# One SBUF tile for staging and factor buffers (15 to 20), one PSUM tile per unit, whole places for the split halves, in an attention and two-MoE kernel

## The chip, the cores and the metric

The kernel runs on one core of a Trainium2 chip. The metric is the device time of one execution in microseconds (us); before the change it is 1255.41 us, the median of three runs (1255.03 to 1257.26).

## What is computed

Three stages follow each other; the output of each is the input of the next. Everything is float32; products on TensorE run as three passes of a value split into a high part and a rest ("hi" and "lo").

```python
# attention: 8 batches, 8 heads, 576 positions in chunks of 64, head size 64
scores = scale * q_c @ k_c.T;  attn = exp(scores - max) / (sum + 1e-9)
x = (attn @ v_c)                                  # 4608 tokens x 512
# first MoE: d_ff = 1024
h = x @ w_in;  e = exp(h - max);  solu = h * e / (sum(e) + 1e-9)
x = layernorm(solu, eps=1e-6) * g_ln @ w_out      # 4608 x 512
# second MoE: d_ff = 2048
h = x @ w2_in;  out = (h * sigmoid(h)) @ w2_out
```

## The kernel before

**Stage one** (attention and the first MoE) goes over 36 tiles of 128 tokens. For a tile, `attend`, `weigh`, `moe_in`, `norm` and `turn_ln` run in turn; four tiles make a block, and `moe_out` multiplies a block by `w_out` and stores it to DRAM (`y1d`). Beside this, `convert` stages pieces of the weights through tiles `st_w` (2 buffers) and `cv` (4 buffers), `w2_mix` forms the sums of weight blocks that stage two needs, and `w2_store` writes them to DRAM.

**Stage two** does the second MoE with seven products in place of eight for 2 x 2 blocks, in both its matrices. Tokens come in 6 groups of 768. For the first matrix a group has 8 **units** `u` (blocks of 128 rows), taken in pairs, and a unit has seven **products** p1, p6, p2, p7, p5, p4, p3, each of 6 matmuls of 384 columns (line 822). In a pair each product is done for both units before the next one. The products gather in PSUM at four places: X (p1, p2), Y (p6, p7), W (p5, p3) and V (p4). Sums are drawn off into **factor buffers** `tmp`, places of 128 x 384 in SBUF: `c_p1` (ACT, line 830), `c_u2` and `c_u3` (DVE, reading Y, lines 833 and 836), `c22` (DVE, reading W between p5 and p3, line 846), `c21` (line 854), `c12` (DVE, reading W after p3, line 862). SiLU is applied on ACT, then `g_sum` (line 869) takes four differences of the results, and every result is stored to DRAM (`gd`, line 827). A buffer comes free when its store has landed. There are 15 of them, made from tiles that stage one no longer needs: `st_w` and `cv` give two each, `ys` and `junk` one each. While the first group's inputs sit in five of those tiles, fewer are there.

At the turn from one token group to the next, four sums of the new inputs (`raw_t`, POOL) and seven splits (`s_split`: ACT line 786, then DVE or POOL line 790) replace the inputs `y1s` one by one, as the old group's products finish with them. The halves of `y1s` lie in groups of ten, so that the third split falls into two tiles and takes two instructions on each engine.

The second matrix follows in the same way (`out_product`, line 910: 6 groups, 7 products, 4 pieces of 12 matmuls), fed by `g_load` from DRAM and `g_split` (ACT line 894, DVE line 896); its weights `w2o` are loaded (line 745) while the last token group's products run.

**What sets the order.** A planner (`Steps`) goes through all steps with given lengths, due times, needs and counts of places, and gives every step a time; the program is written out in the order of those times, engine by engine. Due times come from `NOMINAL`, `START` and others at the end of the file; the strings `Y_ON`, `T_ON`, `UNIT_ON`, `LOW_ON` say on which engine a split or a difference runs. On the chip each engine takes its instructions in that order, and waits that are needed for the data are set by the tile framework: by region for SBUF, and for PSUM by whole tile. Y of both units of a pair is one PSUM tile of two banks (`hy`), and W of both another (`hw`).

Of the kernel before, what the change touches and what calls it, by code (L numbers as in the profile page):

```python
# [136 lines left out]
def stage_one(T, way_out, w2_from, tiles=36, per=4, ahead=2):  # L137
# [45 lines left out]
    for t in range(tiles):  # L183
        b, tt = divmod(t, per)
        x = T[t]
        op("moe_in", (t,), ("PE", 2.73, dict(need=wi[0] + [("xs", t)], take=["h"], due=x + 2.73)),
           ("PE", 2.73, dict(need=wi[1], free=["xs"], give=[("h", t)], due=x + 5.5)))
        held = HELD[t] == "H"
        if held:
            op("hold", (t,), ("ACT", 1.12, dict(need=[("h", t)], take=["hs"], free=["h"], due=x + gap - 0.5, give=[("hs", t)])))  # L190
        op("norm", (t,), ("DVE", 1.23, dict(need=[("hs" if held else "h", t)])), ("ACT", 1.3, dict(take=["u"])),
           ("DVE", 1.51, dict(free=["hs"], port=True, give=[("free", t)]) if held else dict(free=["h"], due=x + gap - 0.5)), ("ACT", 1.34, {}), ("DVE", 0.15, {}),
           ("POOL", 0.85, {}), ("ACT", 1.12, dict(give=[("u", t)])))
# [22 lines left out]
def stage_two(step, start, groups=6, NF=8, tiles=36):  # L216
# [28 lines left out]
    mixed = [("mixed", j, right, k) for j in range(NF) for right in (0, 1) for k in range(4)]  # L245
    all_raw = {"st_w": ([("sp", 0, 3)], [("sp", 0, 4), ("rt", 0, 1)]), "cv": (mixed, [("sp", 0, 5)], [("sp", 0, 6), ("rt", 0, 1)], [("sp", 0, 1), ("rt", 0, 2), ("rt", 0, 3)]), "ys": 2 * ([("stored", end_b, 3)],), "junk": ([("turned", tiles - 1, 1)],)}
    for tag, needs in all_raw.items():
        for n, need in enumerate(needs):
            plan("spare", (tag, n), need, ["tmp"] * (1 if tag in ("ys", "junk") else 2))
    plan("raw_places", (0,), mixed)  # L250
# [6 lines left out]
    for p in range(groups):  # L257
# [83 lines left out]
def chunk_attention_moe_moe(ctx: ExitStack, tc: tile.TileContext, qk, v, w_in, w_out, g_ln, w2_in, w2_out, out):  # L341
# [53 lines left out]
    for kind, src in ((0, lambda f: w2_in[f]), (1, lambda f: w2_out[128 * f:128 * f + 128, :])):  # L395
        for j in range(K2 // 2):
            for f in (j, j + K2 // 2):
                pieces.append(("w2", f, kind, src(f)))
    conv, whole = {}, {}

    early = {}

    def conv_load(i):
# [6 lines left out]
        else:  # L410
            st = sb.tile([128, 2 * CW], I32 if wide else F32, tag="st_w", name="st_w", bufs=2)
        if len(src.shape) > 2:
# [4 lines left out]
    def conv_a(i, apart=False):  # L417

        st = conv[i][0]
        if st.dtype == F32:  # L420
            if pieces[i][0] == "w2":
                conv[i][1] = sb.tile([128, 2, CW], I32, tag="cv", name="cv", bufs=4)
            return
# [5 lines left out]
        else:  # L429
            cv = sb.tile([128, 2, CW], I32, tag="cv", name="cv", bufs=4)  # L430
        conv[i][1] = cv
# [39 lines left out]
    def conv_c(i):  # L471
# [50 lines left out]
    def w2_mix(j, right):  # L522
        top, low = whole.pop(j), whole.pop(j + K2 // 2)
        a, b = (top[:, 1, 256 * i:256 * i + 256].bitcast(F32) for i in (0, 1))
# [114 lines left out]
    def norm(t):  # L639
# [15 lines left out]
        yield  # L655
        junk = sb.tile([128, 2, 512], BF16, tag="junk", name="junk")
        nc.scalar.activation(out=junk, in_=u, func=AF.Square, bias=nmu, scale=1.0, accum_out=ss)
# [19 lines left out]
    def moe_out(b, m):  # L677
# [96 lines left out]
    def s_places(n):  # L774
        t = sb.tile([128, 4096], F32R, tag="ln", name="y1s", bufs=4)[:, 0:3840].rearrange("p (i a f) -> p i a f", i=5, a=2)
        for i in range(5):
            o, kk = divmod(5 * n + i, 2)
            if o < 7:
                sy[o, kk] = (t, i)

    def s_split(p, o):
        src = raw(p, FROM[SEVEN[o]])
        (t0, i0), (t1, i1) = sy[o, 0], sy[o, 1]
        runs = [(t0, i0, 0, 2)] if t0 is t1 else [(t0, i0, 0, 1), (t1, i1, 1, 1)]
        for t, i, k, n in runs:
            nc.scalar.activation(out=t[:, i:i + n, 0, :], in_=src[:, k:k + n], func=AF.Copy)
        yield
        for t, i, k, n in runs:
            hi, lo = (t[:, i:i + n, a, :] for a in (0, 1))
            (nc.vector if Y_ON[o] == "D" else nc.gpsimd).tensor_tensor(out=lo, in0=src[:, k:k + n], in1=hi.bitcast(F32), op=ALU.subtract)  # L790

    def spare(tag, _):
        n, bufs = {"ys": (1, 2), "junk": (1, 1), "st_w": (2, 2), "cv": (2, 4)}[tag]
        t = sb.tile([128, n, HW], F32, tag=tag, name="tmp", bufs=bufs)
        tmp.extend(t[:, i] for i in range(n))

# [170 lines left out]
SUM_ON = 'EDEEEDDEEDDDDDDD'  # L967
# [40 lines left out]
```

## Time and profile before

| | before |
|---|---|
| median of 3 runs | 1255.41 us |
| profiled execution, its own time | 1254.76 us |
| its span, first to last instruction | 1252.8 us |
| TensorE matmul busy | 1221.4 us, 98% of the span |
| TensorE weight load busy | 1115.1 us, 89% |
| VectorE / ScalarE / GpSimd busy | 819.2 (65%) / 637.4 (51%) / 431.4 us (34%) |
| mean granted TensorE clock | 0.998 of full speed |
| DMA queue | 243.33 MB, 60.3% of the 16 engines' time |

Busy time of TensorE is the union of pipelined matmuls, so an engine that is busy may still start matmuls more slowly than it could: the count of matmuls that a stretch holds says more than its busy share. In the views, a bracket behind an instruction is the idle time of its engine before it and what ended that. Stage one fills the span up to about 505 us, the products of stage two run to about 903 us (mixed with stage one up to 533 us and with the second matrix from 891 us), and the second matrix from 891 us to the end.

### The profile page before, as it was taken

Reading aid. Unit: us, or ns where it says so; the run is one execution under the profiler, and the core shown is the slowest. Engines: PE = TensorE matmul, PEld = TensorE weight load, DVE = VectorE, ACT = ScalarE, POOL = GpSimd, SP = SyncE. Lnnn points to the kernel's source line nnn. Section 1 sums busy time; section 2 is a strip of 40 time slices with the busy share of each in tenths; the row PEclk is TensorE's granted clock in tenths of the full one; section 3 lists DMA queues with packets and bytes.
Section 4 is the critical chain, followed back from the end, with each engine's and each line's share of the span. In section 5 each row is a group of like instructions: output and inputs, shape, how many; then the busy total and the mean of one; then the engine's idle time right before and its main releaser. Section 6 shows DMA issues by size and latency. Waiting matters only on the chain. (4 is left out here: it accounts for less than half of the span.)

```text
span 1252.8 us, 22744 instructions
## 1 busy us (share of the span) xinstructions
PE 1221.4 (98%) x8535; PEld 1115.1 (89%) x8535; DVE 819.2 (65%) x1304; ACT 637.4 (51%) x1030; POOL 431.4 (34%) x457
## 2 busy tenths in 40 slices
PE   6999999999999999999999999998999999999998
PEld 3777888888888888899999999998899999999998
DVE  7998877889888544376565656573656555555553
ACT  6776755555555547454343434354555444444441
POOL 1432343343433316556464737366650000000000
PEclk9999999999999999999999999999999999999999
DMA  7343554655654414285656565658898777777772
GB/s 294 127 153 114 170 164 161 218 179 193 202 173 161 139 48 145 83 267 199 232 184 227 193 222 186 233 174 281 272 323 281 213 225 211 220 211 217 223 210 87
DMA packets 137645, 244.77 MB, mean 195 GB/s; under 512 B 15168, under 2 KB 92992, under 8 KB 137536
## 3 DMA queue, kind: packets, MB, share of 16 engines
q1 hardware_dynamic: 137536, 243.33, 60.3%
q8 instruction: 67, 1.10, 0.4%
q14 instruction: 42, 0.34, 0.1%
HBM read 143.66 MB, written 99.61 MB: 194 GB/s over the span
## 5 line engine op out<-in xcount | busy, mean ns | idle before, releaser
L896 DVE TENSOR_TENSOR gs<-gs 128x768 fp32r<-128x768 f32 x168 | 165.8, 988 | 142.3 <-ACT gs L894 142.0
L894 ACT ACTIVATE gs<-gs 128x768 fp32r<-128x768 f32 x168 | 142.2, 847 | 176.9 <-PE h L910 61.0
L627 PE MATMUL h<-wi,xs 128*128 128x512 f32 x864 | 214.6, 397 | 1.7 <-ACT hs L637 1.7
L683 PE MATMUL yp<-lnT,wo 128*128 128x512 f32 x864 | 215.1, 398 | 0.0
L627 PEld LDWEIGHTS h<-wi,xs 128*128 128x128 f32 x864 | 159.3, 188 | 37.7 <-ACT hs L637 3.1
L683 PEld LDWEIGHTS yp<-lnT,wo 128*128 128x128 f32 x864 | 157.6, 188 | 32.2
L822 PE MATMUL h<-y1s,w2t 128*128 128x384 f32 x864 | 163.6, 337 | 0.6 <-DVE y1s L790 0.6
L910 PE MATMUL h<-gs,w2o 128*128 128x384 f32 x864 | 162.4, 337 | 0.6 <-DVE gs L896 0.5
L869 POOL TENSOR_TENSOR tmp<-tmp 128x384 f32<-128x384 f32 x96 | 107.7, 1128 | 135.3 <-DVE tmp L869 96.5
L822 PEld LDWEIGHTS h<-y1s,w2t 128*128 128x128 f32 x864 | 152.6, 189 | 1.2 <-DVE y1s L790 0.9
L910 PEld LDWEIGHTS h<-gs,w2o 128*128 128x128 f32 x864 | 152.1, 188 | 1.2 <-DVE gs L896 0.8
L822 PE MATMUL hw<-y1s,w2t 128*128 128x384 f32 x576 | 111.5, 339 | 8.7 <-DVE tmp L846 8.3
L822 PE MATMUL hy<-y1s,w2t 128*128 128x384 f32 x576 | 109.4, 336 | 2.6 <-DVE tmp L836 2.6
L822 PEld LDWEIGHTS hw<-y1s,w2t 128*128 128x128 f32 x576 | 101.2, 189 | 11.9 <-DVE tmp L846 11.3
L910 PE MATMUL hy<-gs,w2o 128*128 128x384 f32 x576 | 107.3, 335 | 0.3 <-DVE gs L896 0.3
L910 PE MATMUL hw<-gs,w2o 128*128 128x384 f32 x576 | 107.5, 336 | 0.0
L822 PEld LDWEIGHTS hy<-y1s,w2t 128*128 128x128 f32 x576 | 100.9, 188 | 4.1 <-DVE tmp L836 3.9
L910 PEld LDWEIGHTS hy<-gs,w2o 128*128 128x128 f32 x576 | 100.4, 188 | 0.8 <-DVE gs L896 0.8
L910 PEld LDWEIGHTS hw<-gs,w2o 128*128 128x128 f32 x576 | 100.9, 188 | 0.0
L612 ACT ACTIVATE lnT<-tp 128x512 fp32r<-128x512 f32 x72 | 42.7, 598 | 77.6 <-PE tp L672 77.6
L614 DVE TENSOR_TENSOR lnT<-tp,lnT 128x512 fp32r<-128x512 f32 x72 | 49.0, 684 | 38.2 <-ACT lnT L612 37.8
L869 DVE TENSOR_TENSOR tmp<-tmp 128x384 f32<-128x384 f32 x96 | 68.7, 729 | 4.9 <-ACT tmp L864 2.5
(128 smaller groups left out, 1640.7 us busy)
## 6 DMA issues: line engine op xcount, KB each, us to landing
gd<-tmp SPq DMA_DIRECT2D x336, 192.0 KB, 2.1
gs<-gd SPq DMA_DIRECT2D x168, 384.0 KB, 3.7
qk<-in_qk_dram SPq DMA_DIRECT2D x36, 512.0 KB, 4.2
st_w<-in_w_out_dram SPq DMA_DIRECT2D x24, 512.0 KB, 4.1
vt<-in_v_dram SPq DMA_DIRECT2D x36, 256.0 KB, 2.7
y1d<-ys SPq DMA_DIRECT2D x36, 256.0 KB, 2.5
ry<-y1d SPq DMA_DIRECT2D x24, 384.0 KB, 4.1
out_dram<-tmp SPq DMA_DIRECT2D x48, 192.0 KB, 3.8
```

Of the source, the lines that this page charges most:

```text
L612: nc.scalar.activation(out=hi, in_=src, func=AF.Copy)
L614: nc.vector.tensor_tensor(out=lo, in0=src, in1=hi.bitcast(F32), op=ALU.subtract)
L627: nc.tensor.matmul(h_t[t][:, n, :], xs[:, a, kk // 2, 128 * (kk % 2):128 * (kk % 2) + 128], wi[b][kk][:, n * 512:(n + 1) * 512], start=(kk ...
L683: nc.tensor.matmul(yp, wo[a][f // 4][:, f % 4, 128 * m:128 * (m + 1)], lnT[b][c][:, f, :], start=(f == 0 and i == 0), stop=(f == K1 - 1 an ...
L822: nc.tensor.matmul(acc, wt[j, o][:, a, kk, :], t[:, i, c, :], start=start and kk == 0 and n == 0, stop=kk == 1 and n == 2, skip_group_chec ...
L869: (nc.vector if T_ON[n] == "D" else nc.gpsimd).tensor_tensor(out=out, in0=in0, in1=in1, op=ALU.subtract)
L894: nc.scalar.activation(out=dst[:, 0], in_=src, func=AF.Copy)
L896: nc.vector.tensor_tensor(out=dst[:, 1], in0=src, in1=dst[:, 0].bitcast(F32), op=ALU.subtract)
L910: nc.tensor.matmul(acc, w[:, a, 128 * i:128 * i + 128], g[:, c, k, :], start=start and kp == 0 and k == 0 and n == 0, stop=kp == NF // 2 - ...
```

## The change

Staging, conversion, output and junk tiles become one SBUF tile `work` of 7680 columns: six parts of 1024 columns serve stage one's loads (2) and conversions (4) with lists of free parts, two of 512 hold `ys`, one holds `junk`. In stage two the same 7680 columns are 20 factor buffers of 384 columns; the first group's inputs take the first ten until they are split. In PSUM, Y and W of one unit now share a tile of two banks (`hyw`, one for even units, one for odd units), in place of Y of both and W of both. Each half (hi, lo) of a split input is one contiguous place of 768 columns, so that every split is one instruction. The planner is told of the new places, of a need of p5 for `c_u3`, and of the two PSUM tiles' last readers in stage one; its numbers at the end of the file are new, and with them the order on all engines.

```diff
-    all_raw = {"st_w": ([("sp", 0, 3)], [("sp", 0, 4), ("rt", 0, 1)]), "cv": (mixed, [("sp", 0, 5)], ...
+    plan("spare", (10, 6), mixed, ["tmp"] * 6)
+    plan("spare", (16, 4), [("stored", end_b, 3), ("stored", end_b, 2), ("turned", tiles - 1, 1)], ["tmp"] * 4)
+    for n, need in enumerate(([("sp", 0, 3)], [("sp", 0, 4), ("rt", 0, 1)], [("sp", 0, 5)], ...
+        plan("spare", (2 * n, 2), need, ["tmp"] * 2)
...
-               ("POOL", 2.1, dict(give=[("sp", p, o)])) if Y_ON[o] == "P" else ("DVE", 1.25 if o != 2 else 1.7, ...
+               ("POOL", 2.1, dict(give=[("sp", p, o)])) if Y_ON[o] == "P" else ("DVE", 1.1, ...
...
-                need += {"p2": [("c_p1", u)], "p7": [("c_u2", u)], "p3": [("c22", u)]}.get(name, [])
+                need += {"p2": [("c_p1", u)], "p7": [("c_u2", u)], "p5": [("c_u3", u)], "p3": [("c22", u)]}.get(name, [])
+                if p == 0 and o == 1 and u < 2:
+                    need.append(("free" if u == 0 else "xs", tiles - 1))
...
+    work = sb.tile([128, 7680], F32, name="work")
+    cv_free, st_free = [0, 1, 2, 3], [4, 5]
+    def part(n, dtype):
+        w = work[:, 1024 * n:1024 * n + 1024]
+        return w if dtype == F32 else w.bitcast(dtype)
...
-        ys = sb.tile([128, BLK], F32, tag="ys", name="ys", bufs=2)
+        n = 6144 + 512 * (m % 2)
+        ys = work[:, n:n + 512]
...
     def s_split(p, o):
         src = raw(p, FROM[SEVEN[o]])
-        (t0, i0), (t1, i1) = sy[o, 0], sy[o, 1]
-        runs = [(t0, i0, 0, 2)] if t0 is t1 else [(t0, i0, 0, 1), (t1, i1, 1, 1)]
-        for t, i, k, n in runs:
-            nc.scalar.activation(out=t[:, i:i + n, 0, :], in_=src[:, k:k + n], func=AF.Copy)
+        hi, lo = sy[o, 0], sy[o, 1]
+        nc.scalar.activation(out=hi, in_=src, func=AF.Copy)
...
+    def spare(n, count):
+        tmp.extend(work[:, HW * i:HW * i + HW] for i in range(n, n + count))
...
-                if at_ not in bank:
-                    bank[at_] = ps.tile([128, 2, 512], F32, tag={"w": "h", "y": "sx"}[at_], name="h" + at_)
-                bank[u, at_] = bank[at_][:, u % 2, 0:HW]
+                if u % 2 not in bank:
+                    bank[u % 2] = ps.tile([128, 2, 512], F32, tag=("h", "sx")[u % 2], name="hyw")
+                bank[u, at_] = bank[u % 2][:, "yw".index(at_), 0:HW]
...
-FIRST = [-128.33, 3, 21.63, 3.75, 5.92, 13.32, 4.31, 12.18, 4.58, 11.93, 5.72, 6.85, 5.13]
-NOMINAL = [sum(FIRST[:t + 1]) + 13.48 * max(0, t + 1 - len(FIRST)) for t in range(36)]
+FIRST = [-83.81, 3, 24.83, 3, 8.92, 13.48, 4.31, 12.84, 4.51, 11.93, 5.72, 6.44, 5.13]
+NOMINAL = [sum(FIRST[:t + 1]) + 13.52 * max(0, t + 1 - len(FIRST)) for t in range(36)]
-W2_FROM = 14
+W2_FROM = 12
-Y_ON = 'PPDDPDP'
-T_ON = 'DDPP'
-UNIT_ON = 'PPPPPDPPPPPPPPPDPPDPDPDPPPDD'
-START = 543.9
+Y_ON = 'PDDDPDP'
+T_ON = 'PDPP'
+UNIT_ON = 'PPPPDDPDPPDPDPDPPPDDDPDPPPDD'
+START = 575.8
-LOW_ON = 'EEEPDDDPPPEPEPDP'
+LOW_ON = 'EEEPDDDPPPEPPPDE'
```

So `g_sum`'s first difference goes from DVE to POOL (three of four run there now), the second split from POOL to DVE (four of seven are on DVE now), and twelve in place of seven of the first weight splits are on DVE.

**First place: TensorE at the turn between two token groups.** The rows are the end of the new group's first pair and the start of its second; `hw` or `hyw` with a DVE wait is p3, `h2` is p1 of the next pair, `hy` or the later `hyw` is p6. Before:

```order
L822 MATMUL h2_7075<-y1s_5703,w2t_5528 128x384 [waits Activation_49]
L822 MATMUL h2_7075<-y1s_5703,w2t_5528 128x384 x5
L822 MATMUL hw_5926<-y1s_5913,w2t_5457 128x384 [waits DVE_49]
L822 MATMUL hw_5926<-y1s_5913,w2t_5457 128x384 [waits Pool_49]
L822 MATMUL hw_5926<-y1s_5913,w2t_5457 128x384 x4
L822 MATMUL h2_7092<-y1s_5703,w2t_5570 128x384 [waits Activation_49]
L822 MATMUL h2_7092<-y1s_5703,w2t_5570 128x384 x5
L822 MATMUL hy_5809<-y1s_5703,w2t_5528 128x384 x6
L822 MATMUL hy_5809<-y1s_5703,w2t_5580 128x384 [waits DVE_49]
L822 MATMUL hy_5809<-y1s_5703,w2t_5580 128x384 x5
L822 MATMUL hw_5926<-y1s_5913,w2t_5506 128x384 [waits DVE_49]
```

With the change:

```order
L829 MATMUL hyw_5648<-y1s_5747,w2t_5304 128x384 [waits DVE_49]
L829 MATMUL hyw_5648<-y1s_5747,w2t_5304 128x384 [waits Pool_49]
L829 MATMUL hyw_5648<-y1s_5747,w2t_5304 128x384 x4
L829 MATMUL hyw_5674<-y1s_5747,w2t_5353 128x384 [waits DVE_49]
L829 MATMUL hyw_5674<-y1s_5747,w2t_5353 128x384 x5
L829 MATMUL h2_6930<-y1s_5546,w2t_5375 128x384 [waits Activation_49]
L829 MATMUL h2_6930<-y1s_5546,w2t_5375 128x384 x5
L829 MATMUL h2_6941<-y1s_5546,w2t_5416 128x384 [waits Activation_49]
L829 MATMUL h2_6941<-y1s_5546,w2t_5416 128x384 x5
L829 MATMUL hyw_5648<-y1s_5546,w2t_5375 128x384 [waits DVE_49]
L829 MATMUL hyw_5648<-y1s_5546,w2t_5375 128x384 x5
L829 MATMUL hyw_5674<-y1s_5546,w2t_5426 128x384 [waits DVE_49]
```

Before, the products of two pairs are mixed here: p6 of the next pair's even unit comes ahead of a DVE step that reads the same tile `hy`, and p6 of the odd unit waits for that step. Now p3 of both units comes first, and each p6 waits for the last reader of its own unit's tile.

**Second place: TensorE within a token group, from p7 to p3 of a pair.** Before:

```order
L822 MATMUL hy_5809<-y1s_5704,w2t_5638 128x384 [waits DVE_49]
L822 MATMUL hy_5809<-y1s_5704,w2t_5638 128x384 x5
L822 MATMUL hy_5809<-y1s_5704,w2t_5748 128x384 x6
L822 MATMUL hw_5926<-y1s_5704,w2t_5718 128x384 x6
L822 MATMUL hw_5926<-y1s_5704,w2t_5748 128x384 x6
L822 MATMUL h2_7334<-y1s_5913,w2t_5718 128x384 x6
L822 MATMUL h2_7344<-y1s_5913,w2t_5910 128x384 x6
```

With the change:

```order
L829 MATMUL hyw_5648<-y1s_5547,w2t_5382 128x384 [waits DVE_49]
L829 MATMUL hyw_5648<-y1s_5547,w2t_5382 128x384 x5
L829 MATMUL hyw_5674<-y1s_5547,w2t_5448 128x384 [waits DVE_49]
L829 MATMUL hyw_5674<-y1s_5547,w2t_5448 128x384 x5
L829 MATMUL hyw_5648<-y1s_5547,w2t_5409 128x384 [waits DVE_49]
L829 MATMUL hyw_5648<-y1s_5547,w2t_5409 128x384 x5
L829 MATMUL hyw_5674<-y1s_5547,w2t_5448 128x384 [waits DVE_49]
L829 MATMUL hyw_5674<-y1s_5547,w2t_5448 128x384 x5
L829 MATMUL h2_7027<-y1s_5747,w2t_5409 128x384 x6
L829 MATMUL h2_7038<-y1s_5747,w2t_5454 128x384 x6
```

The products stand in the same order, but p5, which waited for nothing, now waits for DVE: its tile is the one that `c_u3` reads. Between p7 of a unit and its p5 stands one product of the other unit.

**Third place: TensorE where the second matrix starts** (`gs` rows), from p5 or p4 of the last pair on. Before:

```order
L822 MATMUL h_9158<-y1s,w2t 128x384 x6
L822 MATMUL h_9170<-y1s,w2t 128x384 x6
L910 MATMUL h_9181<-gs,w2o 128x384 x6
L910 MATMUL h_9182<-gs,w2o 128x384 x6
L910 MATMUL h_9181<-gs,w2o 128x384 x6
L910 MATMUL h_9182<-gs,w2o 128x384 x6
L910 MATMUL h_9181<-gs,w2o 128x384 x6
L910 MATMUL h_9182<-gs,w2o 128x384 x6
L822 MATMUL hw<-y1s,w2t 128x384 x6
L910 MATMUL h_9181<-gs,w2o 128x384 x6
L910 MATMUL h_9182<-gs,w2o 128x384 x6
L822 MATMUL hw<-y1s,w2t 128x384 x6
```

With the change:

```order
L829 MATMUL h_8961<-y1s,w2t 128x384 x6
L829 MATMUL h_8973<-y1s,w2t 128x384 x6
L829 MATMUL hyw<-y1s,w2t 128x384 x18
L917 MATMUL h_9014<-gs,w2o 128x384 x6
L917 MATMUL h_9015<-gs,w2o 128x384 x6
L917 MATMUL h_9014<-gs,w2o 128x384 x6
L917 MATMUL h_9015<-gs,w2o 128x384 x6
L829 MATMUL hyw<-y1s,w2t 128x384 x6
L917 MATMUL h_9014<-gs,w2o 128x384 x6
L917 MATMUL h_9015<-gs,w2o 128x384 x6
```

One p3 has moved ahead of the second matrix; the other stands behind 24 of its matmuls.

## Rows read from the trace of the kernel before

**Rows 1.** The profile page, busy time by engine, TensorE:

```profile
PE 1221.4 (98%) x8535; PEld 1115.1 (89%) x8535; DVE 819.2 (65%) x1304; ACT 637.4 (51%) x1030; POOL 431.4 (34%) x457
```

**Rows 2.** Windows, TensorE: stretch, its length, busy (matmuls), clock, DMA share, GB/s.

```profile
592.00:612.00 20.00, 18.36 (x104) 1.00 0.71 244
657.00:677.00 20.00, 18.86 (x107) 1.00 0.69 244
716.00:736.00 20.00, 18.68 (x106) 1.00 0.66 229
778.00:798.00 20.00, 18.88 (x107) 1.00 0.68 242
853.00:891.00 38.00, 33.56 (x181) 0.96 0.77 257
891.00:941.00 50.00, 47.57 (x266) 1.00 0.93 316
1000.00:1020.00 20.00, 20.00 (x117) 1.00 0.81 230
```

**Rows 3.** Waits of TensorE, 500 to 850, then 850 to 940: total, times, longest.

```profile
PE hw L822 <- DVE tmp L846: 2.6, 4, 1.0
PE hy L822 <- DVE tmp L836: 2.6, 4, 0.7
...
PE hw L822 <- DVE tmp L846: 5.6, 3, 3.7
```

**Rows 4.** Timeline of TensorE, 650 to 680: start, length, line, count.

```profile
657.06 3.31 PE L822 MATMUL h<-y1s,w2t 128*128 128x384 f32 x18
660.86 1.31 PE L822 MATMUL hw<-y1s,w2t 128*128 128x384 f32 x6 [0.49 <-DVE tmp L846]
...
664.92 1.33 PE L822 MATMUL hy<-y1s,w2t 128*128 128x384 f32 x6 [0.65 <-DVE tmp L836]
...
667.14 2.26 PE L822 MATMUL h<-y1s,w2t 128*128 128x384 f32 x12
...
673.40 2.24 PE L822 MATMUL h<-y1s,w2t 128*128 128x384 f32 x12
...
677.56 2.26 PE L822 MATMUL h<-y1s,w2t 128*128 128x384 f32 x12
```

**Rows 5.** Timeline of VectorE, the same stretch.

```profile
660.25 0.56 DVE L846 TENSOR_TENSOR tmp<-hw,tmp 128x384 f32<-128x384 f32 x1 [2.08 <-DMA gd<-tmp]
...
664.31 0.56 DVE L836 TENSOR_TENSOR tmp<-hy,tmp 128x384 f32<-128x384 f32 x1 [1.55 <-PE hy L822]
...
675.68 0.56 DVE L854 TENSOR_TENSOR tmp<-h,tmp 128x384 f32<-128x384 f32 x1 [0.48 <-PE h L822]
```

**Rows 6.** Timeline of TensorE, 838 to 945, the passage to the second matrix.

```profile
858.95 2.17 PE L822 MATMUL hw<-y1s,w2t 128*128 128x384 f32 x6 [3.69 <-DVE tmp L846]
...
891.16 6.43 PE L910 MATMUL h<-gs,w2o 128*128 128x384 f32 x36
898.88 1.31 PE L822 MATMUL hw<-y1s,w2t 128*128 128x384 f32 x6 [1.29 <-DVE tmp L846]
...
937.01 2.19 PE L910 MATMUL h<-gs,w2o 128*128 128x384 f32 x11 [0.55 <-DVE gs L896]
```

**Rows 7.** Timeline of VectorE, the same stretch.

```profile
858.33 0.56 DVE L846 TENSOR_TENSOR tmp<-hw,tmp 128x384 f32<-128x384 f32 x1 [6.71 <-DMA gd<-tmp]
...
898.26 0.56 DVE L846 TENSOR_TENSOR tmp<-hw,tmp 128x384 f32<-128x384 f32 x1 [5.06 <-DMA gd<-tmp]
```

**Rows 8.** Instructions of lines 869 and 790: duration in ns, least, median, most.

```profile
L869 DVE TENSOR_TENSOR tmp<-tmp x96: 543/557/2191, 544.6 to 908.0; 128x384 f32<-128x384 f32 x96
L869 POOL TENSOR_TENSOR tmp<-tmp x96: 994/1021/1737, 547.4 to 925.6; 128x384 f32<-128x384 f32 x96
...
L790 DVE TENSOR_TENSOR y1s<-ry,y1s x24: 871/1716/2332, 507.2 to 833.3; 128x384 fp32r<-128x384 f32 x12, 128x768 fp32r<-128x768 f32 x12
```

**Rows 9.** Groups by line and shape: count, busy us, mean ns, idle before.

```profile
L833 DVE TENSOR_TENSOR tmp<-hy,tmp 128x384 f32<-128x384 f32 x48 | 25.6, 553 | 24.4 <-ACT y1s L786 10.9 <-PE hy L822 10.4 <-issue 2.2
...
L614 DVE TENSOR_TENSOR xs<-sx,xs 128x512 fp32r<-128x512 f32 x36 | 24.6, 684 | 6.8 <-ACT xs L612 6.8
```

More of the change, by code (lines that the diff above doesn't have):

```diff
@@ L191, in stage_one @@
         op("norm", (t,), ("DVE", 1.23, dict(need=[("hs" if held else "h", t)])), ("ACT", 1.3, dict(take=["u"])),
-           ("DVE", 1.51, dict(free=["hs"], port=True, give=[("free", t)]) if held else dict(free=["h"], due=x + gap - 0.5)), ("ACT", 1.34, {}), ("DVE", 0.15, {}),
+           ("DVE", 1.51, dict(free=["hs"], port=True, give=[("free", t)]) if held else dict(free=["h"], due=x + gap - 0.5, give=[("free", t)])), ("ACT", 1.34, {}), ("DVE", 0.15, {}),
            ("POOL", 0.85, {}), ("ACT", 1.12, dict(give=[("u", t)])))
@@ L245, in stage_two @@
     mixed = [("mixed", j, right, k) for j in range(NF) for right in (0, 1) for k in range(4)]
[L246 to L249, printed above, removed]
+    plan("spare", (10, 6), mixed, ["tmp"] * 6)
+    plan("spare", (16, 4), [("stored", end_b, 3), ("stored", end_b, 2), ("turned", tiles - 1, 1)], ["tmp"] * 4)
+    for n, need in enumerate(([("sp", 0, 3)], [("sp", 0, 4), ("rt", 0, 1)], [("sp", 0, 5)], [("sp", 0, 6), ("rt", 0, 1)], [("sp", 0, 1), ("rt", 0, 2), ("rt", 0, 3)])):
+        plan("spare", (2 * n, 2), need, ["tmp"] * 2)
     plan("raw_places", (0,), mixed)
@@ L410, in conv_load @@
         else:
-            st = sb.tile([128, 2 * CW], I32 if wide else F32, tag="st_w", name="st_w", bufs=2)
+            conv["st", i] = st_free.pop(0)
+            st = part(conv["st", i], I32 if wide else F32)
         if len(src.shape) > 2:
@@ L421, in conv_a @@
             if pieces[i][0] == "w2":
-                conv[i][1] = sb.tile([128, 2, CW], I32, tag="cv", name="cv", bufs=4)
+                conv["cv", i] = cv_free.pop(0)
+                conv[i][1] = part(conv["cv", i], I32).rearrange("p (a f) -> p a f", a=2)
             return
@@ L429, in conv_a @@
         else:
-            cv = sb.tile([128, 2, CW], I32, tag="cv", name="cv", bufs=4)
+            conv["cv", i] = cv_free.pop(0)
+            cv = part(conv["cv", i], I32).rearrange("p (a f) -> p a f", a=2)
         conv[i][1] = cv
@@ L655, in norm @@
         yield
-        junk = sb.tile([128, 2, 512], BF16, tag="junk", name="junk")
+        junk = work[:, 7168:7680].bitcast(BF16).rearrange("p (a f) -> p a f", a=2)
         nc.scalar.activation(out=junk, in_=u, func=AF.Square, bias=nmu, scale=1.0, accum_out=ss)
@@ L754, in raw_places @@
         if p == 0:
-            for i, tag in enumerate(("st_w", "st_w", "cv", "cv", "cv")):
-                raw_y[i] = sb.tile([128, 2, HW], F32, tag=tag, name="ry0", bufs=2 if tag == "st_w" else 4)
+            for i in range(5):
+                raw_y[i] = work[:, 768 * i:768 * i + 768].rearrange("p (k f) -> p k f", k=2)
         else:
@@ L774, in s_places @@
     def s_places(n):
-        t = sb.tile([128, 4096], F32R, tag="ln", name="y1s", bufs=4)[:, 0:3840].rearrange("p (i a f) -> p i a f", i=5, a=2)
+        t = sb.tile([128, 4096], F32R, tag="ln", name="y1s", bufs=4)[:, 0:3840].rearrange("p (i k f) -> p i k f", i=5, k=2)
         for i in range(5):
-            o, kk = divmod(5 * n + i, 2)
-            if o < 7:
-                sy[o, kk] = (t, i)
+            sy[divmod(5 * n + i, 2)] = t[:, i]
     def s_split(p, o):
         src = raw(p, FROM[SEVEN[o]])
-        (t0, i0), (t1, i1) = sy[o, 0], sy[o, 1]
-        runs = [(t0, i0, 0, 2)] if t0 is t1 else [(t0, i0, 0, 1), (t1, i1, 1, 1)]
-        for t, i, k, n in runs:
-            nc.scalar.activation(out=t[:, i:i + n, 0, :], in_=src[:, k:k + n], func=AF.Copy)
+        hi, lo = sy[o, 0], sy[o, 1]
+        nc.scalar.activation(out=hi, in_=src, func=AF.Copy)
         yield
[L788 to L795, printed above, removed]
+        (nc.vector if Y_ON[o] == "D" else nc.gpsimd).tensor_tensor(out=lo, in0=src, in1=hi.bitcast(F32), op=ALU.subtract)
+    def spare(n, count):
+        tmp.extend(work[:, HW * i:HW * i + HW] for i in range(n, n + count))
     def take(key):
@@ L819, in product @@
         for kk in range(2):
-            t, i = sy[o, kk]
             for n, (a, c) in enumerate(PASSES):
-                nc.tensor.matmul(acc, wt[j, o][:, a, kk, :], t[:, i, c, :], start=start and kk == 0 and n == 0,
+                nc.tensor.matmul(acc, wt[j, o][:, a, kk, :], sy[o, c][:, kk, :], start=start and kk == 0 and n == 0,
                                  stop=kk == 1 and n == 2, skip_group_check=not start)
```

18 lines of the change are left out of this document (11 added, 7 removed).

## The prediction

> **What bounds the kernel now.** The page comes first: TensorE has matmuls in flight for 98% of the span, every other engine 65% at most [rows 1]. Only time in which TensorE starts matmuls late can be won, so the views to read are those that show missing matmuls. In the second matrix a 20 us window holds 117 [rows 2], and 60 of the first matrix take 667.14 to 677.56, 10.42 us: 0.1737 us each [rows 4]. By that pace the four windows at the turns between token groups, with 104, 107, 106 and 107, lack 13 + 10 + 11 + 10 = 44 matmuls, 7.6 us. The stretch 853 to 891 could hold 220 and holds 181: 39 lack, 6.8 us, and its clock is 0.96. From 891 to 941, 266 stand where 289 fit: 23 lack, 4.0 us [rows 2]. Together 18.4 us: all that a change in the order of waits can win in stage two.
>
> The waits name the causes [rows 3]. From 500 to 850 two kinds last, four times each: p3 for `c22`, 2.6 us in all, and p6 for `c_u3`, 2.6 us. The timelines show one turn. `c22` stands 2.08 us on VectorE until a store (`gd`) has landed and its buffer is free [rows 5]; TensorE has p4 of both units and one product more to do in the meantime and then loses 0.49 us [rows 4]. Then p6 of the odd unit waits 0.65 us for `c_u3` [rows 4, 5], which itself waited 1.55 us for p6 of the *next* pair's even unit, since both units share the tile `hy`: a dependence of the tile, not of the data. At the passage `c22` waits 6.71 us and, last, 5.06 us for landings [rows 7]; TensorE loses 3.69 and 1.29 us [rows 6], 5.6 us with a third [rows 3]. After the longest wait six matmuls take 2.17 us, where six after 0.49 or 1.29 us take 1.31 [rows 4, 6]: the granted clock fell, which is most of what the waits alone don't explain of the 6.8.
>
> **Term 1, the turns: 7.6 us, take -5.6.** The way from product to landed store is read at the turn: p5 of that unit ended 6 matmuls before 657.06, at 656.0; the order puts the latest product of the stored result 12 matmuls earlier, at 653.9; the landing was at 660.2 [rows 5]. That is 6.3 us. In the new order the result whose store frees the buffer stands at least 54 matmuls (9.4 us) ahead, counted at all four turns, so the buffer is free 3 us before it is asked for. The wait for `c_u3` goes too: in the first piece of order p3 of both units comes ahead of the new pair's p6, and no step of DVE needs a product behind the one that waits for it. What comes next: p6 of a new unit now waits for `c12` of the old one, its tile's last reader, and in a turn DVE has four splits instead of three, each from 0.87 to 2.33 us [rows 8]. TensorE has one to two products (1.04 to 2.08 us) of other work before it needs `c12`. If a split lies ahead of it the stall is 0 (a 0.87 us split) to about 1.2 us (2.33); I take 0.5 per turn, since about half the splits are short, 2.0 in all: -5.6, ends -7.6 and -2.8.
>
> On that lengthening: the least and median of those splits, 871 and 1716 ns, and VectorE's differences, 543 to 2191 ns [rows 8], differ with the same form of instruction, while the sums that read PSUM average 553 ns over 48 [rows 9]. The Trainium skill, SBUF — State Buffer, section "Who interferes with whom", has a rule for it: a VectorE instruction with two SBUF inputs and a GpSimd instruction that reads SBUF exclude each other for a whole instruction. The trace agrees; by that rule alone, every split that meets a GpSimd operation would take the long time, the stall would be 1.2 in each turn, and the total 2.8 us higher than mine.
>
> **Term 2, 853 to 891: 6.8 us, take -6.3.** Here stores land later. For the last `c22`, p5 ended 18 matmuls before 891.16, at 888.0, and the landing was at 898.2 [rows 6, 7]: 10.2 us from a result with no matmul between. For the first, the stall began at 858.95 - 3.69 = 855.26, p5 ended 18 matmuls earlier at 852.1, and the stored result stands 24 to 30 matmuls (4.2 to 5.2 us) before that: 10.4 to 11.4 us. The new order puts 60 to 114 matmuls there, 10.4 to 19.8 us, and p4 of the pair still covers 2 us. So the two waits go, and with them the fall of the clock; 0.5 us I leave for one landing that is late. Ends -6.8 and -3 (stores slower by a third: one wait stays).
>
> **Term 3, 891 to 941: 4.0 us, take -1.6 + 1.0.** The last `c22` asks for a result 30 matmuls back, and p3, behind 24 matmuls of the second matrix and a p3, waits for it 30 later: 10.4 us against 10.2 and 0.6 for `c22` and its hand-over. The 1.29 us wait shrinks to some tenths and the restart goes with it: -1.6. But the DMA share here is 0.93 [rows 2] and the second matrix already waits 0.55 us for its inputs [rows 6]: what is won before 891 brings the same bytes (w2o, `gd`, `gs`) closer together. Transfers of the 50 us at 0.93 leave 3.5 us of slack; about 12 us are taken out of the time before. Ends 0 and +8 (rival one); I take +1.0, because only the `gs` loads of the first group lie on the path and the loads of w2o before them now start earlier too.
>
> **Term 4, the new wait of p5: take +0.7.** In the second piece of order p5 waits for `c_u3` of its own unit. From p7's end there is one product of room, 1.04 us. The way takes 0.20 us to VectorE (twelve matmuls from 673.40 end at 675.48, the reader starts at 675.68), 0.56 for the sum [rows 4, 5], 0.05 back (664.31 + 0.56 to 664.92): 0.81. So 0.23 us remain, 24 pairs, two units each. Whatever stands in VectorE's way for over 0.23 us is a stall. VectorE has 48 x 0.557 us of differences less than before, which went to POOL at 1.021 us each [rows 8]; I take 0.03 us per pair. Ends 0 and 24 x 0.8 = 19 (rival two). The Trainium skill, PSUM — Partial Sum Buffer, section "PSUM bank collisions raise a hardware error", asks for a guard by bank; p5's half of the tile is another bank than the one that `c_u3` reads, so by it the 0.7 would fall away. The order shows the wait for the whole tile all the same; no row here shows a guard by bank.
>
> **Term 5, stage one: take +0.8.** The order now has only eight transposes between the last `attend` and `moe_in` of an early tile, where more stood before. ACT and then VectorE split what `moe_in` needs; VectorE's part is 0.684 us [rows 9], ACT's I take as as long, with two hand-overs of 0.2: 1.8 us. No row gives the eight transposes alone; between all of the way hidden (0) and none (1.8) I take 0.8, once; ends 0 and 2.
>
> **At nothing:** staging parts in one tile (the same loads and conversions beside a full TensorE, whose list up to 50 us is unchanged); whole places for halves (one split instruction fewer on ACT and one fewer on VectorE or POOL per turn); the number of matmuls (equal); POOL's 48 x 1.02 us more, at 34% busy [rows 1], as long as the differences stay behind `c12` on the path; the second matrix behind 941, whose waits keep over 3 us of room in the order.
>
> **Sum.** -5.6 - 6.3 - 1.6 + 1.0 + 0.7 + 0.8 = -11.0. The profiled execution took 1254.76 us (span 1252.8), so 1243.8; the median of runs stands 0.65 above it: **1244.4 us**.
>
> **Rivals.**
> *One: the passage is bound by DMA.* At a share of 0.93 [rows 2] the saved 8 us before 891 come back as waits for `gs` and w2o after it; terms 1, 4 and 5 remain: -5.6 + 0.7 + 0.8 = -4.1, about 1251. For it: 316 GB/s against 230 to 257 elsewhere. Against: the share falls to 0.77 just before, and loads can move there. Chance 0.12.
> *Two, slower: `c_u3` late within the groups.* With two units in a tile, each pair exposes two chains of 0.81 us to a VectorE that also runs splits and differences, which POOL stretches to 2.19 us [rows 8], and POOL has 49 us more. If TensorE loses 0.8 us in each of 24 pairs, that is +19 on -11: 1263. It decides when `c_u3` starts over 0.23 us late; the kernel becomes slower when the mean lateness passes 0.23 + 11/24 = 0.69 us. Against: within a group no wait of TensorE lasts now [rows 3], and `c_u3` starts freely. Chance 0.08.
> *Three: the turns stay.* Splits on VectorE hold `c12` by 1.2 us or more and p6 with it; the turns win 1 or 2 us in place of 5.6, 1248 to 1249. For it: four of seven splits there. Chance 0.13.
> *Four: it doesn't do what it says.* If landings, not the count of buffers, set the pace, more buffers only shift the wait: 1255. Against: POOL and VectorE have room [rows 1], stores wait for no buffer. Chance 0.05.
>
> **How the numbers follow.** The forecast has 0.62. Its best case takes term 1 to 3 nearly whole and 4 and 5 at nothing, -16.5: 1238.9, a little lower with the spread of the runs: 1237. Upward the range takes in rivals one and three and stops at 1253, leaving rivals two and four and their neighbours out. A measurement of this kernel can tell some 0.2%, 2.5 us, from no change. Faster by more: forecast, one and three, less their upper ends, 0.85; same 0.08; slower 0.07.
>
> **What would show it.** Right: windows at the turns with 114 matmuls or more, no wait of `c22` for `gd` at turns, clock 1.00 in the passage, p5's waits for `c_u3` below 1 us in all. Wrong: p5 or p6 with waits of half a us in most pairs (two); `gs` and w2o waits of several us after the start of the second matrix (one); p6 waiting for `c12` behind a `y1s` split (three); `c22` still behind `gd` (four).

## The result, and the profile after

The changed kernel takes 1238.23 us (median of 4 runs, 1237.28 to 1239.64), the kernel before in the same series 1256.01 us (4 runs, 1255.03 to 1257.26): a ratio of 0.9859, 95% interval 0.9842 to 0.9876. The forecast was 1244.4 us with a range of 1237 to 1253; the gain is 17 to 18 us where 11 were expected. The profiled execution took 1239.64 us, span 1237.5, which is 15.1 us under the profiled execution before.

The page of the changed kernel, busy time by engine (beside [rows 1]):

```profile
PE 1218.4 (98%) x8535; PEld 1115.8 (90%) x8535; DVE 815.5 (66%) x1262; ACT 638.2 (52%) x1024; POOL 467.8 (38%) x493
```

TensorE's busy time hardly moved, 3 us; the count of matmuls in a stretch shows the gain. Windows of TensorE in the changed kernel, the stretches of [rows 2] and one more:

```profile
592.00:612.00 20.00, 19.99 (x115) 1.00 0.76 268
657.00:677.00 20.00, 20.00 (x116) 1.00 0.63 233
716.00:736.00 20.00, 20.00 (x117) 1.00 0.68 251
778.00:798.00 20.00, 20.00 (x116) 1.00 0.65 240
853.00:891.00 38.00, 36.00 (x198) 0.96 0.88 294
891.00:941.00 50.00, 50.00 (x289) 1.00 0.93 304
520.00:540.00 20.00, 20.00 (x103) 1.00 0.42 128
```

The turns are full (117 is the most). 853 to 891 lacks 22 of 220; 891 to 941 is full, and its DMA share is still 0.93. The last window was not priced: before it reads

```profile
520.00:540.00 20.00, 19.45 (x98) 1.00 0.42 123
```

so 5 matmuls, 0.9 us, were won there: before, the first group's products waited 0.6 us for a split of `y1s`, and now they don't. Waits of TensorE from 500 to 940 in the changed kernel (who waited for whom: total, times, longest), beside [rows 3]; it is the whole list:

```profile
PE hyw L829 <- DVE work L853: 2.0, 1, 2.0
```

No p5 waits for `c_u3`, no p6 for `c12`. VectorE's timeline at the turn that [rows 5] showed before (it now comes some 4 us earlier), start and length in us, with the idle time and its end in the bracket:

```profile
651.27 0.56 DVE L843 TENSOR_TENSOR work<-hyw,work 128x384 f32<-128x384 f32 x1 [2.52 <-PE hyw L829]
...
653.37 0.56 DVE L853 TENSOR_TENSOR work<-hyw,work 128x384 f32<-128x384 f32 x1 [0.50 <-PE hyw L829]
...
655.45 0.56 DVE L853 TENSOR_TENSOR work<-hyw,work 128x384 f32<-128x384 f32 x1 [0.48 <-PE hyw L829]
```

For `c_u3` (L843) and both `c22` (L853) VectorE now stands idle until TensorE's product is done, 2.52, 0.50 and 0.48 us; before, TensorE stood for them. The one wait left is at the passage. TensorE, VectorE, GpSimd and the DMA queue of SyncE there:

```profile
861.41 2.24 PE L829 MATMUL hyw<-y1s,w2t 128*128 128x384 f32 x12
...
873.96 2.27 PE L829 MATMUL hyw<-y1s,w2t 128*128 128x384 f32 x12
878.23 1.31 PE L829 MATMUL hyw<-y1s,w2t 128*128 128x384 f32 x6 [2.00 <-DVE work L853]
879.38 5.90 PE L917 MATMUL h<-gs,w2o 128*128 128x384 f32 x24
```

```profile
862.65 0.56 DVE L869 TENSOR_TENSOR work<-hyw,work 128x384 f32<-128x384 f32 x1 [0.48 <-PE hyw L829]
...
865.24 1.35 DVE L876 TENSOR_TENSOR work<-work 128x384 f32<-128x384 f32 x1 [0.99 <-POOL work L876]
...
877.62 0.56 DVE L853 TENSOR_TENSOR work<-hyw,work 128x384 f32<-128x384 f32 x1 [4.50 <-DMA gd<-work]
```

```profile
863.17 4.44 SPq L761 DMA_DIRECT2D w2o<-w2od  x7
867.70 2.57 SPq L834 DMA_DIRECT2D gd<-work  x4
...
872.15 1.74 SPq L834 DMA_DIRECT2D gd<-work  x3
```

The `c22` of the last pair's even unit waits 4.50 us for a landing. Its buffer holds a second difference (865.24, after GpSimd's first), whose p3 ended six matmuls behind 861.41, at 862.45. Counted in the order, its store is the second of the three issued from 872.15, at 872.87, behind seven loads of `w2o`, four stores and a load of `gs`, and it landed by 877.57: 15.1 us from product to landing, where 10.2 to 11.4 were read before. The difference was done at 866.59, 4.1 us behind the product; 6.3 us passed until the store was issued, and 4.7 until it had landed. What the issue stood for is one of those loads: the one issued at 866.67 landed at 872.80, 0.07 us before the store was issued. SyncE's waits from 867 to 874 say the same (total, times, longest):

```profile
SPq L834 <- DMA w2o<-w2od: 2.0, 4, 1.1
```

TensorE loses 2.0 us, and the 24 matmuls after it take 5.90 us, where 24 from 892.42 on take 4.33. From 880 to 900 the window holds 109 at a granted clock of 0.93, a mean of the clock's two levels (1.2 and 2.4 GHz). Together 22 matmuls, 3.8 us.

### The profile page after: what moved, and what is told of

Its sections match the earlier page's. It is cut to its first block, busy times and chain, and to the rows that moved or that the text cites. A ratio compares the mean times of both kernels' runs of the same rounds, so it can differ in the third digit from the quotient of the medians.

```text
span 1237.5 us, 22712 instructions
## 1 busy us (share of the span) xinstructions
PE 1218.4 (98%) x8535; PEld 1115.8 (90%) x8535; DVE 815.5 (66%) x1262; ACT 638.2 (52%) x1024; POOL 467.8 (38%) x493
## 4 chain that ended last, share of the span: by engine, by line
PE 95%; DVE 3%; DMA 1%; ACT 1%; issue 0%; POOL 0%; SPq 0%; DVEq 0%; ACTq 0%; POOLq 0%
PE hyw L917 16%; PE yp L698 16%; PE h L642 16%; PE hyw L829 16%; PE h L917 12%; PE h L829 12%; PE tp L687 2%; PE sx L588 2%; PE sx L595 1%; PE pp L620 1%; DMA w2o<-w2od 0%; DMA gd<-work 0%; DVE e L607 0%; ACT hs L652 0%; DMA qk<-in_qk_dram 0%; DVE mx L605 0%
## 5 line engine op out<-in xcount | busy, mean ns | idle before, releaser
L829 PE MATMUL hyw<-y1s,w2t 128*128 128x384 f32 x1152 | 215.3, 336 | 2.0 <-DVE work L853 2.0
L917 PE MATMUL hyw<-gs,w2o 128*128 128x384 f32 x1152 | 210.9, 335 | 0.0
L829 PEld LDWEIGHTS hyw<-y1s,w2t 128*128 128x128 f32 x1152 | 201.8, 188 | 3.2 <-DVE work L853 2.3
L917 PEld LDWEIGHTS hyw<-gs,w2o 128*128 128x128 f32 x1152 | 200.9, 188 | 0.2 <-issue 0.2
L876 POOL TENSOR_TENSOR work<-work 128x384 f32<-128x384 f32 x144 | 161.0, 1136 | 77.8 <-ACT work L871 67.9
L616 POOL TENSOR_TENSOR e<-e,sm 128x512 f32<-128x512 f32 x36 | 40.5, 1124 | 76.1 <-DVE sm L614 67.3
L855 ACT ACTIVATE work<-work 128x384 f32<-128x384 f32 x48 | 25.2, 524 | 84.4 <-DVE work L853 84.3
L876 DVE TENSOR_TENSOR work<-work 128x384 f32<-128x384 f32 x48 | 52.0, 1091 | 15.6 <-POOL work L876 15.6
L843 DVE TENSOR_TENSOR work<-hyw,work 128x384 f32<-128x384 f32 x48 | 26.5, 555 | 54.0 <-PE hyw L829 54.0
L549 POOL TENSOR_TENSOR work<-work 128x256 f32<-128x256 f32 x64 | 50.4, 808 | 29.0 <-DVE work L497 27.8
```

The lines of the kernel that those rows point to most:

```text
L549: nc.gpsimd.tensor_tensor(out=out_, in0=in0, in1=in1, op=op)
L616: nc.gpsimd.tensor_tensor(out=e, in0=e, in1=sm.to_broadcast([128, HP, 2, CH]), op=ALU.mult)
L829: nc.tensor.matmul(acc, wt[j, o][:, a, kk, :], sy[o, c][:, kk, :], start=start and kk == 0 and n == 0, stop=kk == 1 and n == 2, skip_group ...
L843: nc.vector.tensor_tensor(out=take((u, "u3")), in0=bank[u, "y"], in1=c_t[u, "u2"], op=ALU.add)
L876: (nc.vector if T_ON[n] == "D" else nc.gpsimd).tensor_tensor(out=out, in0=in0, in1=in1, op=ALU.subtract)
L917: nc.tensor.matmul(acc, w[:, a, 128 * i:128 * i + 128], g[:, c, k, :], start=start and kp == 0 and k == 0 and n == 0, stop=kp == NF // 2 - ...
```

## The experiments

All times stand beside runs of the kernel before on the same chip (its medians there were 1255.45 us for the first four kernels below, 1256.36 for the next three and 1256.72 for the last three).

**The parts one by one, planned with the numbers of before.** Three kernels have the changed code with `START`, `FIRST`, `NOMINAL`, `W2_FROM`, `Y_ON`, `T_ON`, `UNIT_ON` and `LOW_ON` of before. The first is that alone:

```diff
-START = 575.8
+START = 543.9
-T_ON = 'PDPP'
+T_ON = 'DDPP'
...
```

> The changed kernel with the numbers and engine strings of before (START, FIRST, Y_ON, T_ON, UNIT_ON, LOW_ON): 20 buffers and one PSUM tile per unit alone, planned anew. Theory A (the waits for landed stores go because more buffers are there): no buffer is asked for less than 11 us behind the product of its stored result at the turns, and 13 us at the passage; so no wait of c22 for gd, about 1235 to 1239 us, as fast as the change or up to 3 us faster. Theory B (the new numbers are what pays): about 1250. Theory C (both are needed): 1242 to 1246.

Measured: 1236.68 us, ratio 0.9851 (0.9836 to 0.9866). Theory A held: no `c22` makes TensorE wait, and the passage is full.

```profile
853.00:891.00 38.00, 38.00 (x221) 1.00 1.02 351
891.00:941.00 50.00, 49.29 (x279) 1.00 0.90 297
```

The new numbers bring nothing that can be seen; the tiles alone give the whole gain. The second has 15 buffers:

```diff
-    plan("spare", (10, 6), mixed, ["tmp"] * 6)
-    plan("spare", (16, 4), [("stored", end_b, 3), ("stored", end_b, 2), ("turned", tiles - 1, 1)], ["tmp"] * 4)
+    plan("spare", (10, 2), mixed, ["tmp"] * 2)
+    plan("spare", (16, 3), [("stored", end_b, 3), ("stored", end_b, 2), ("turned", tiles - 1, 1)], ["tmp"] * 3)
```

> As the run with 20 buffers and the numbers of before, but with 15 buffers (5 more parts of the tile lie idle): the PSUM tile per unit alone. Theory A: c22 takes buffers 3.1 us behind the product at each turn where a landing takes 6.3, so the waits stay or grow, and p5 and p6 now wait behind c22 too: 1254 to 1266 us. Theory that the tile of PSUM pays (the wait of p6 for c_u3, 0.65 us with its restart at each turn): 1249 to 1252.

Measured: 1249.61 us, 0.9958 (0.9944 to 0.9973). Theory A is wrong in one half here. Windows of this kernel at two turns and at the passage:

```profile
657.00:677.00 20.00, 20.00 (x116) 1.00 0.69 254
716.00:736.00 20.00, 20.00 (x117) 1.00 0.71 262
...
853.00:891.00 38.00, 34.29 (x186) 0.95 0.70 229
891.00:941.00 50.00, 46.50 (x260) 1.00 0.95 320
```

The turns are full with 15 buffers: the PSUM tile per unit is enough for them. Theory A's other half did come: `c22` still waits for a landed store at four turns, 1.1 to 1.5 us, and the order still puts p1 of the next pair ahead of p3. At one turn, VectorE, then TensorE:

```profile
656.25 0.56 DVE L853 TENSOR_TENSOR work<-hyw,work 128x384 f32<-128x384 f32 x1 [1.15 <-DMA gd<-work]
```

```profile
654.89 3.31 PE L829 MATMUL h<-y1s,w2t 128*128 128x384 f32 x18
```

These 18 matmuls (p4 of one unit, p1 of the next two) cover it; p3 of both units comes next, and only then p6, so that no p6 stands for a `c_u3`. The passage is as bad as before. VectorE and TensorE there:

```profile
849.06 0.56 DVE L843 TENSOR_TENSOR work<-hyw,work 128x384 f32<-128x384 f32 x1 [7.38 <-DMA gd<-work]
```

```profile
849.67 4.95 PE L829 MATMUL hyw<-y1s,w2t 128*128 128x384 f32 x18 [2.32 <-DVE work L843]
```

18 matmuls take 4.95 us, where 18 at a turn take 3.31 [rows 4]: the clock again. The third has 20 buffers and the PSUM tiles of before:

```diff
-                if u % 2 not in bank:
-                    bank[u % 2] = ps.tile([128, 2, 512], F32, tag=("h", "sx")[u % 2], name="hyw")
-                bank[u, at_] = bank[u % 2][:, "yw".index(at_), 0:HW]
+                if at_ not in bank:
+                    bank[at_] = ps.tile([128, 2, 512], F32, tag={"w": "h", "y": "sx"}[at_], name="h" + at_)
+                bank[u, at_] = bank[at_][:, u % 2, 0:HW]
...
-                need += {"p2": [("c_p1", u)], "p7": [("c_u2", u)], "p5": [("c_u3", u)], "p3": [("c22", u)]}.get(name, [])
+                need += {"p2": [("c_p1", u)], "p7": [("c_u2", u)], "p3": [("c22", u)]}.get(name, [])
```

> As the run with 20 buffers and the numbers of before, but with the PSUM tiles of before (Y of both units, W of both) and without the planner's need of p5 for c_u3: the buffers alone. Theory A: the order has no p6 behind a c_u3 of the same tile any more, since the pairs need not be mixed when buffers are there: 1235 to 1240 us. Theory that the tile of PSUM is half of it: waits of p6 for c_u3 stay at four turns, 1240 to 1244.

Measured: 1239.63 us, 0.9879 (0.9861 to 0.9897). Its windows:

```profile
657.00:677.00 20.00, 20.00 (x117) 1.00 0.64 238
716.00:736.00 20.00, 20.00 (x117) 1.00 0.66 243
...
853.00:891.00 38.00, 38.00 (x219) 1.00 1.00 336
891.00:941.00 50.00, 48.18 (x273) 1.00 0.90 292
```

The turns are full here too: with buffers at hand the planner no longer mixes two pairs, and no p6 stands behind a `c_u3` of the same tile. One wait of 0.7 us for a `c22` is left, at 555 us, within the first group. With one of 0.6 us for a split of `y1s` and 1.9 us for `gs` (0.4 with the tile per unit), it covers most of the 3.0 us that this kernel lies above the first. So either part alone clears the four turns' windows, and only the buffers clear the passage (the kernel before differs from the other three in its staging tiles and in its third split too):

| with the numbers of before | Y of both, W of both | one tile per unit |
|---|---|---|
| 15 buffers | 1255.45 (before) | 1249.61 |
| 20 buffers | 1239.63 | 1236.68 |

**The wait that is left.** One kernel only puts the first difference back on VectorE:

```diff
-T_ON = 'PDPP'
+T_ON = 'DDPP'
```

> The changed kernel with the first difference of g_sum back on VectorE (DDPP), all else as changed. Theory: the one wait left, 2.0 us of c22 for a store at the passage with the fall of the clock behind it (22 matmuls, 3.8 us), comes from the first difference waiting on GpSimd behind splits of w2o, which holds the second difference and its store; then the passage is full, 1234 to 1236 us. Rival (the transfers at a DMA share of 0.94 hold the store): same wait, within 1 us of the change. Second rival: VectorE's 48 differences more make c12 late at the turns: slower by 1 to 4 us.

Measured: 1236.08 us, 0.9844 (0.9827 to 0.986). The passage is full, but something comes back behind it:

```profile
853.00:891.00 38.00, 38.00 (x220) 1.00 0.99 342
891.00:941.00 50.00, 48.85 (x277) 1.00 0.88 288
```

22 matmuls won, 12 lost, 1.7 us by the pace. Seven `w2o` loads stand in the queue here as well; but the planner, given earlier differences, hands this `c22` another buffer, whose product lies some 40 us back. So it is not shown that GpSimd's difference was late, only that the buffer was. The other way is to move the loads:

```diff
+        if 28 <= pos < 42:
+            need = need + [("t", NF * groups - i, n) for i in (3, 4) for n in range(4)]
```

> The changed kernel with seven loads of w2o (the third batch) planned behind the four differences of the last pair but one, so that its stores go ahead of them on the DMA queue; T_ON stays PDPP. Theory (the last wait of c22 comes from the queue: seven loads of 256 KB stand before the store that frees its buffer): the wait of 2.0 us and the fall of the clock go, 22 matmuls or 3.8 us in the passage; some 1 to 2 us may come back as waits for gs: 1235 to 1237 us against 1238.2. Rival (the first difference on GpSimd is late): the wait stays at 1 to 2 us, 1237 to 1239.

Measured: 1239.99 us, 0.987 (0.9853 to 0.9887), a miss in the total: not faster than the change. But its first half held. Windows:

```profile
853.00:891.00 38.00, 38.00 (x221) 1.00 0.92 309
891.00:941.00 50.00, 46.62 (x256) 0.97 0.90 295
```

Waits of TensorE, 500 to 940:

```profile
PE hyw L919 <- DVE work L944: 2.5, 1, 2.5
PE hyw L919 <- DVE gs L905: 0.9, 2, 0.5
```

With the queue in another order and the first difference still on GpSimd, the stores of the pair before land in time and the passage is full, though the planner now hands this `c22` a buffer asked for only 54 matmuls, 9.4 us, behind its product: the loads ahead of the store were enough to make it late. The price came some 40 us later: the draw-off of the second matrix (`o_sum`, L944) stands on VectorE behind `gs` splits that wait for late loads, TensorE loses 2.5 us, the clock falls, and 33 matmuls are gone.

**What comes back behind the passage.** The kernel with `DDPP`, and the last four `w2o` loads later:

```diff
+        if pos >= 48:
+            need = need + [("od", 0, 1, 3)]
```

> The run with DDPP, and the last four w2o loads (needed some 48 us after the second matrix starts) planned behind its second product. Theory (the 12 matmuls, 2.1 us, that 891 to 941 lacks with DDPP are waits for gs behind w2o on the queue, which is what the saved time gave back): they go in part, 1234 to 1235.5 us against 1236.1. Rival (gs is late because its stores gd land late, not because of w2o): no change, 1235.8 to 1236.5.

Measured: 1235.43 us, 0.9834 (0.9817 to 0.985). The window 891 to 941 holds 281 in place of 277: 0.7 us, and the medians differ by as much. But they come from two chips, and the intervals of the two ratios overlap, so the gain is not clear of noise. Of two waits for `gs`, 0.96 and 0.17 us, one of 1.04 us stays: it is not shown that `w2o` was the longer one's cause.

**Whole places for the halves**, undone:

```diff
-        nc.scalar.activation(out=hi, in_=src, func=AF.Copy)
+        runs = [slice(0, 2)] if o != 2 else [slice(0, 1), slice(1, 2)]
+        for k in runs:
+            nc.scalar.activation(out=hi[:, k], in_=src[:, k], func=AF.Copy)
...
```

> The changed kernel with the third split of y1s in two instructions on each engine as before, in the order as planned. Theory: whole places alone bring nothing, since the turns have room: within 0.7 us of the change (1237.5 to 1239). Rival (the turns are short of VectorE time): c12 late and p6 with it at five turns, 1 to 3 us slower.

Measured: 1236.68 us (1235.99 to 1239.71), 0.9848 (0.983 to 0.9866): no slower, so whole places bring nothing. It came out 0.8 us under the range expected, and why leads to the next point: its profile has the same wait, and the window after it a clock of 1.00:

```profile
PE hyw L832 <- DVE work L856: 1.8, 1, 1.8
```

```profile
880.00:900.00 20.00, 20.00 (x116) 1.00 0.90 297
```

**The change and two faster variants on one chip.**

> The changed kernel itself, beside the two fastest variants on the same chip. Theory: its runs lie on two levels about 2 us apart, 1237.3 and 1239.4, by whether the last wait of c22 (about 2 us) is followed by a fall of the granted clock; the mean against the kernel before is 0.985 to 0.987.

Measured: 1238.58 us, 0.9855 (0.9838 to 0.9872); its four runs are 1237.33, 1237.82, 1239.35 and 1239.44. The profiled one, 1239.35, has the same wait of 1.8 us, and then

```profile
880.00:900.00 20.00, 20.00 (x108) 0.92 0.84 269
```

8 matmuls less than in the kernel above with an equal wait: after it the clock fell in one and not in the other, and 8 x 0.1737 = 1.4 us of the 2 us between the levels is that. Only the profiled executions have a trace; that the other runs on the upper level are slower by the same thing is not shown.

> DDPP with the last four w2o loads behind the second product of the second matrix, again. Theory (the wait at the passage and the clock's fall are gone): all runs on one level, 2 to 4 us below the change on the same chip. Rival (the difference seen was one of chips): within 1 us of the change.

Measured: 1235.38 us, 0.9833 (0.9818 to 0.9847); its four runs lie between 1235.36 and 1235.43. It is 3.2 us below the change on the same chip, the fastest seen, and its runs agree within 0.1 us, where the change's spread over 2.1.

> 20 buffers and a PSUM tile per unit with the numbers of before, and the last four w2o loads later as in the run beside it. Theory: like that run, within 1.5 us of it, since both have no buffer asked for under 13 us at the passage; the numbers do not matter. If the waits for gs go in part as there: 1235 to 1236.5.

Measured: 1235.88 us, 0.9837 (0.9822 to 0.9851): 0.5 us above the other (both have `DDPP`), so the remaining numbers at the end of the file make half a microsecond here. The later loads do not shorten the waits for `gs` here: 1.0 us, where the first kernel of this section had 0.4.

## Why the prediction was right, and where its sizes were off

**The forecast held and the four rivals fell:** no turn stayed, nothing was late on VectorE within the groups, the passage was not given back in the change itself, and the buffers did what they were for. Two of the signs named for it did not come clean: the clock in the passage was 0.96, not 1.00, and one `c22` was still behind `gd`. By terms, in the two profiled executions:

| term | predicted | measured |
|---|---|---|
| 1, turns | -5.6 | -7.6 (44 matmuls lacking, now 4 at most, the count's own grain) |
| 2, passage 853 to 891 | -6.3 | (39 - 22) x 0.1737 = -3.0 |
| 3, passage 891 to 941 | -1.6 + 1.0 = -0.6 | 23 x 0.1737 = -4.0 |
| 4, p5 behind `c_u3` | +0.7 | 0 |
| 5, stage one | +0.8 | +0.1 |
| not priced: 520 to 540; the first matmul (4.80 us, before 4.49) | 0 | -0.9; +0.3 |
| sum | -11.0 | -15.1 |

The medians differ by 17.8 us; what is beyond 15.1 is where the profiled executions lie among their runs: before, 1.2 us under the median of four; after, 1.4 us over it.

**Term 1** was mis-sized by what was left in: half a microsecond at each turn for `c12` behind the splits. Nothing was lost there; the splits (0.95 to 2.3 us) fall into the time in which VectorE waits for products. The term took 0.87 us for a short split; that is half a split's least time, since 12 of the 24 in [rows 8] have 384 columns, and a whole one takes 0.95 at least after the change. And its account of the cause was too simple. I had `c22`'s landing and the shared tile as two losses, each with its own cure; the kernels with one part each show the windows at the turns full. With the tile per unit alone, `c22`'s wait stays and TensorE has other products to do meanwhile; with the buffers alone, the pairs are no longer mixed and no p6 meets a `c_u3`. What the two orders have in common is that p3 of both units stands ahead of the next pair's p6.

**Terms 2 and 3** came out right as a sum and wrong one by one, and that the errors of 3.3 and 3.4 us cancel each other is luck. The waits of 3.69 and 0.65 us went, as argued. The third, of the last pair's even unit, was to shrink from 1.29 us to "some tenths" and is 2.0. Two steps failed there. The first is the cover: the 24 matmuls of the second matrix that term 3 counts stand before the odd unit's p3, whose `c22` did come in time; the even unit's p3 is the one that moved ahead of the second matrix, and the p4 on whose 2 us term 2 counts stands ahead of p5 in this pair (third place, with the change). The second is the landing time, taken over from before as 10.2 to 11.4 us. In the new order it was 15.1, behind seven loads in the queue, while the buffer was asked for 72 matmuls, 12.5 us, behind its product. The clock took 1.8 us more. So 853 to 891 won 3.0 us, the end that term 2 had given for "stores slower by a third". What made up for it is that 891 to 941 lost nothing at all, where 3.4 was to stay. The waits for `gs` that the prediction feared do come in the variants that clear the passage (8 to 16 matmuls lacking there), and not in the change. That its own stall keeps it from them is likely and not shown: the three executions with the stall, of two kernels, all hold 289.

**Term 4** fell since VectorE is ahead of its products. The page's group of `c_u3` (count, busy us, mean ns, idle before):

```profile
L843 DVE TENSOR_TENSOR work<-hyw,work 128x384 f32<-128x384 f32 x48 | 26.5, 555 | 54.0 <-PE hyw L829 54.0
```

In 48 of them VectorE stood 54.0 us for TensorE, over 1 us each. The margin of 0.23 us was enough in all 24 pairs: weight loads stood 0.7 us in all for `c_u3`, and no matmul did.

**Term 5** was seen and offset. The new wait is 1.2 us (0.8 taken), but a wait of 1.1 us for GpSimd's part of a softmax, in the stretch 60 to 130 before, is not there after the change:

```profile
PE pp L605 <- POOL e L601: 1.1, 1, 1.1
```

```profile
PE h L642 <- ACT xs L627: 1.2, 1, 1.2
```

The kernels with the numbers of before have the first and not the second: it is the numbers that exchange them.

## What to carry to other kernels

When a wait is for a place to come free, count how much work of the bound engine lies between the product that goes into the place and the moment it is asked for, and compare it with the whole way to the landed store, queue included; that way is not a constant, since it grew from 6.3 to 15.1 us, and 10.4 of the 15.1 passed before the store was issued, 6.3 of them behind other transfers. Before giving each of two waits at one spot a cure of its own, ask whether one order makes both. And once a passage is cleared, look at the next resource in line: here 8 to 16 matmuls behind it then went to waits for `gs`, and moving four loads that were not needed for another 48 us gave back 0.7 us at most.

## What was not expected of the hardware

The clock's fall after a wait is not settled by the wait alone: after 1.8 us of TensorE standing still the next 20 us were granted 1.00 in one execution and 0.92 in another of an almost equal kernel, with 116 against 108 matmuls. After 0.49 and 1.29 us [rows 4, 6] it did not fall; after 2.32 (15 buffers) and 3.69 it did. The four runs of the change lie on two levels in both series, near 1237.4 and 1239.4 us.

VectorE's differences became slower as more of them had work of GpSimd beside them: the 96 of before had a median of 557 ns [rows 8], the 48 after

```profile
L876 DVE TENSOR_TENSOR work<-work x48: 544/1222/2137, 547.0 to 895.5; 128x384 f32<-128x384 f32 x48
```

while `c_u3`, which reads one operand from PSUM, stays at 555 ns. The traces tell the two cases apart: before, 57 of the 96 had no instruction of GpSimd beside them, and these took 543 to 560 ns; the other 39 took up to 2191. After, 45 of the 48 had one. Of the 48 `c_u3` after the change, 35 had one too, and none took over 559 ns. The rule in the Trainium skill, SBUF — State Buffer, section "Who interferes with whom", says that a VectorE instruction with two SBUF inputs contends with a GpSimd instruction that reads SBUF, and the trace agrees. No product waits for these differences directly, but one lay on the path to the wait that is left: the difference at 865.24 took 1.35 us, 0.8 more than alone, out of the 15.1.
